# One searched order for all five engines, zero matmuls at the start, and half copies by DMA, in a chunk-selecting attention with a gated MLP

## The chip, the core and the metric

The kernel runs on one core of one Trainium2 chip. A core has a matrix engine (TensorE, PE in the profile; its weight loads are PEld), a vector engine (VectorE, DVE), a scalar engine (ScalarE, ACT), GpSimd (POOL) and SyncE (SP), which here only issues DMA transfers. The engines run side by side, each through its own queue in order, and wait for each other on semaphores. On-chip memory is SBUF; TensorE writes its results to PSUM, which has eight banks. The metric is the device time of the whole program in microseconds.

## The reference, cut to what matters

The input is q, k and v of shape (4, 8, 768, 64): batch, heads, tokens, head dimension. Attention looks at six of the 24 chunks of 32 keys, chosen for each query by an upper bound of its scores in the chunk.

```python
k_min, k_max = chunk minima and maxima of k            # 24 chunks of 32 keys
ub = sum(maximum(q * k_min, q * k_max), axis=-1)       # (B, H, S, 24)
ub = where(causal, ub, -1e9)
top_chunks = argsort(ub)[..., -6:]
scores = q @ k.T / 8
scores = where(selected chunk and causal, scores, -1e9)
attn = softmax(scores)
x = attn @ v                                           # heads side by side: (4, 768, 512)

h = maximum(x @ w_in, 0)                               # (4, 768, 1024)
u, v = h[..., :512], h[..., 512:]
v_n = (v - mean(v)) / sqrt(var(v) + 1e-6)
v_s = w_spatial @ v_n + b_spatial                      # over the tokens
out = (u * v_s) @ w_out                                # (4, 768, 512), float32
```

## The kernel before

The kernel works on 16 pairs of heads, four pairs to a batch. A pair goes through preparation (transposes, bounds, selection), scores, exp, values and normalisation. When the four pairs of a batch are done, its MLP is mixed with the attention of the batches that follow.

The selection is folded into the scores matmul. The operand of a head, `kh`, has the transposed k in 64 partitions and in the other 64 the constant `expand`, which is -30000 where a chunk's row meets that chunk's keys. The other operand, `a`, has q and, for each chunk, a one where the chunk was not selected. So both heads of a pair come from one 128-partition transpose and are then split in halves.

```python
def k_transpose(self):                      # six 128x128 transposes into a PSUM bank
    ...
def k_max(self):                            # DVE, from PSUM; k_min likewise, negated
    nc.vector.tensor_reduce(self.kmm[:, 0, :], self.kT..., axis=AX.X, op=Alu.max)

def k_bounds(self):                         # two copies of 64 partitions
    for hi, (d0, d1) in enumerate(HALF):
        copy = nc.gpsimd.tensor_copy if 2 <= self.i < 4 else nc.scalar.copy
        s0, s1 = HALF[1 - hi]
        copy(self.km[d0:d1, :, hi], self.kmm[s0:s1])

def k_operand(self, hi):                    # half of kT, PSUM -> kh, once for each head
    d0, d1 = HALF[1 - hi]
    copy = nc.scalar.copy if self.i < 1 else nc.vector.tensor_copy
    copy(self.kh[hi][d0:d1], self.kT[d0:d1])

def bounds(self):
    mm(ub[:, 0:(NQT - 1) * W], lhsT=sub_chunk, rhs=later, start=True, stop=False)   # 240 columns
    for qi in range(1, NQT):
        for m in range(2):
            mm(ub[:, (qi - 1) * W:qi * W], lhsT=self.rq[:, m, ...], rhs=self.km[:, m]..., ...)

# then: ten MAX8 on DVE, select() (DVE, is_lt against the sixth), transposes of q with the selection
# into PSUM, and a_copy() by ACT or DVE; from pair 8 on one DMA transpose does both

def scores(self, hi, g):                    # 12 groups a pair, three PSUM banks
    for si, (t, q0, n, col) in enumerate(TILES[g]):
        mm(sc[:, col:col + n], lhsT=self.kh[hi][:, t * P:(t + 1) * P], rhs=self.a[...], ...)
    nc.scalar.activation(out=self.e[hi][...], in_=sc[:, 0:width], func=Act.Exp, scale=scale)
```

Loads of q, k, v and the weights are issued by GpSimd and convert float32 to float16. The k and q buffers and the v buffers are rings of three. `kh` is a ring of four.

```python
for hi, (d0, d1) in enumerate(HALF):        # init_kh: the constant half, on ACT
    nc.scalar.copy(kh_ring[i][hi][d0:d1, :], expand)
```

The order comes from a table of "beats": each step is put at a beat, and the steps are issued beat by beat. Only for the first beats is the order of TensorE's queue kept as written; everywhere else a scheduler may move instructions.

```python
at(t0 - 22, p.k_max)
at(t0 - 21, p.q_transpose)
at(t0 - 20, p.k_min)
... (cut)
with tc.manual_schedule(engines={mybir.EngineType.PE}):
    for beat in sorted(b for b in beats if b < 6):
        ...
for beat in sorted(beats):
    ...
```

Of the kernel before, what the change touches and what calls it, by code (L numbers as in the profile page):

```python
# [16 lines left out]
P = 128  # L17
CHUNK = 32
# [28 lines left out]

@with_exitstack
def kernel(
# [12 lines left out]
    B, H, S, D = q.shape  # L62
# [4 lines left out]
    NQT = S // P  # L67
    NDO = DM // P
    KO = DH // P
    HP = H // 2  # L70
    NPAIR = B * HP
    CPT = P // CHUNK
    scale = 1.0 / math.sqrt(D)
    mm = nc.tensor.matmul

# [4 lines left out]
    ps_sc = ctx.enter_context(tc.psum_pool(name="ps_sc", bufs=3))  # L80
    ps_tr = ctx.enter_context(tc.psum_pool(name="ps_tr", bufs=1))
    ps_acc = ctx.enter_context(tc.psum_pool(name="ps_acc", bufs=1))
    ps_ml = ctx.enter_context(tc.psum_pool(name="ps_ml", bufs=3))

    def ml_tile():
        return ps_ml.tile([P, 512], F32, tag="mlp", name="mlp")
# [3 lines left out]

    BEATS = 12
    beats = defaultdict(list)

    def at(beat, fn, *args):
        beats[beat].append((fn, args))

    HALF = ((0, D), (D, 2 * D))


    NB = 4
    v_ring = [ring.tile([P, 4, NQT, D + 2], F16, name=f"vt{i}") for i in range(3)]
    qs_ring = [ring.tile([P, 2, NQT, 4, D], F16, name=f"qs{i}") for i in range(3)]
    km_ring = [ring.tile([P, 2, 2, NCH], F16, name=f"km{i}") for i in range(2)]
    kh_ring = [[ring.tile([P, S], F16, name=f"kh{i}_{hi}") for hi in range(2)] for i in range(NB)]
    identity = cp.tile([P, P], F16)
    tri = cp.tile([P, P], F16)
    sub_chunk = cp.tile([P, P], F16)
    later = cp.tile([P, (NQT - 1) * 2 * NCH], F16)  # L110
    expand = cp.tile([D, S], F16)
    eps_t = cp.tile([P, 1], F32)

    def init_identity():
        nc.vector.memset(identity, 0.0)
        nc.gpsimd.affine_select(out=identity, in_=identity, compare_op=Alu.not_equal, fill=1.0,
                                base=0, channel_multiplier=1, pattern=[[-1, P]])

    def init_ring(i):

        nc.vector.memset(qs_ring[i][:, :, :, 0:4:3, :], 0.0)

    def init_small():
        nc.vector.memset(km_ring[0], 0.0)
        nc.vector.memset(km_ring[1], 0.0)
        nc.vector.memset(eps_t, 1e-6)
        for t in v_ring:
            nc.vector.memset(t[:, :, :, D:D + 2], 1.0)

    def init_expand():  # L130

        nc.vector.tensor_scalar(expand.rearrange("d (c s) -> d c s", s=CHUNK),
                                in0=identity[0:D, 0:NCH].unsqueeze(2).to_broadcast([D, NCH, CHUNK]),
                                scalar1=NEG, scalar2=None, op0=Alu.mult)
        nc.vector.tensor_copy(sub_chunk.rearrange("d (c s) -> d c s", s=CHUNK),
                              identity[:, 0:CPT].unsqueeze(2).to_broadcast([P, CPT, CHUNK]))

    def init_masks():

        nc.gpsimd.memset(later, 0.0)  # L140
        lv = later.rearrange("p (t h c) -> p t h c", h=2, c=NCH)
        nc.gpsimd.affine_select(out=lv, in_=lv, compare_op=Alu.is_ge, fill=NEG, base=CPT,
                                channel_multiplier=1, pattern=[[CPT, NQT - 1], [0, 2], [-1, NCH]])
# [4 lines left out]
    def init_kh(i):  # L148
        for hi, (d0, d1) in enumerate(HALF):
            nc.scalar.copy(kh_ring[i][hi][d0:d1, :], expand)  # L150


    W = 2 * NCH
    xT = {}
    tiles = {}

    class Pair:
        def __init__(self, i):
            self.i = i
            self.b, self.hp = divmod(i, HP)  # L160
            self.heads = [4 * (self.hp // 2) + self.hp % 2 + 2 * hi for hi in range(2)]
            self.qs = qs_ring[i // 2 % 3][:, i % 2]
            self.kh, self.km = kh_ring[i % NB], km_ring[i % 2]
            self.e = {}

        def k_transpose(self):
            if self.i < 16:
                self.kT = kT = ps_ml.tile([P, S], F16, tag="mlp", name="kTp")
                for t in range(NQT):
                    nc.tensor.transpose(kT[:, t * P:(t + 1) * P], self.k[:, t], identity)  # L170
            else:
                self.kT = sb.tile([P, S], F16, tag="kT", name="kT", bufs=3)
                nc.sync.dma_start_transpose(out=self.kT.rearrange("d (t s) -> d t s", s=P),
                                            in_=self.k.rearrange("p t h d -> p (t h d)"))

        def k_max(self):
            self.kmm = sb.tile([P, 2, NCH], F16, tag="kmm", name="kmm")
            nc.vector.tensor_reduce(self.kmm[:, 0, :], self.kT.rearrange("d (c ch) -> d c ch", ch=CHUNK),  # L178
                                    axis=AX.X, op=Alu.max)

        def k_min(self):
            nc.vector.tensor_reduce(self.kmm[:, 1, :], self.kT.rearrange("d (c ch) -> d c ch", ch=CHUNK),  # L182
                                    axis=AX.X, op=Alu.min, negate=True)

        def k_bounds(self):
            for hi, (d0, d1) in enumerate(HALF):
                copy = nc.gpsimd.tensor_copy if 2 <= self.i < 4 else nc.scalar.copy
                s0, s1 = HALF[1 - hi]
                copy(self.km[d0:d1, :, hi], self.kmm[s0:s1])

        def k_operand(self, hi):
            d0, d1 = HALF[1 - hi]
            copy = nc.scalar.copy if self.i < 1 else nc.vector.tensor_copy
            copy(self.kh[hi][d0:d1], self.kT[d0:d1])  # L194

        def trans_tile(self):

            if self.b == 0:
                return ps_ml.tile([P, S], F16, tag="mlp", name="trm")
            return ps_tr.tile([P, S], F16, tag="tr", name="tr")  # L200

        def q_transpose(self):
            self.tr = self.trans_tile()
            for t in range(1, NQT):
                nc.tensor.transpose(self.tr[:, t * P:(t + 1) * P], self.qs[:, t, 1:3, :], identity)  # L205

        def q_parts(self, m):
            if m == 0:
                self.rq = sb.tile([P, 2, S], F16, tag="rq", name="rq")
                nc.vector.tensor_scalar(self.rq[:, 0, P:S], in0=self.tr[:, P:S], scalar1=0.0, scalar2=None, op0=Alu.max)  # L210
            elif self.i < 1:
                nc.scalar.activation(self.rq[:, 1, P:S], self.tr[:, P:S], func=Act.Relu, scale=-1.0)
# [4 lines left out]
        def bounds(self):  # L217
            ub = self.ub = ps_tr.tile([P, 512], F32, tag="tr", name="ub")
            mm(ub[:, 0:(NQT - 1) * W], lhsT=sub_chunk, rhs=later, start=True, stop=False)
            for qi in range(1, NQT):  # L220
                for m in range(2):
                    mm(ub[:, (qi - 1) * W:qi * W], lhsT=self.rq[:, m, qi * P:(qi + 1) * P],  # L222
                       rhs=self.km[:, m].rearrange("p h c -> p (h c)"), start=False, stop=(m == 1 and qi == NQT - 1))

        def top(self, step):
            ub = self.ub
            if step == 0:
                self.max8 = sb.tile([P, NQT - 1, 2, 8], F32, tag="max8", name="max8")
            for qi in (1, 2, 3) if step == 0 else (4, 5):
                for hi in range(2):  # L230
                    c0 = (qi - 1) * W + hi * NCH
                    nc.vector.max(self.max8[:, qi - 1, hi, :], ub[:, c0:c0 + CPT * (qi + 1)])  # L232

        def select(self):
            flat = self.qs[:, 1:NQT]
            sel = bass.AP(flat.tensor, flat.offset, [list(flat.ap[0]), [4 * D, NQT - 1], [3 * D, 2], [1, NCH]])
            nc.vector.tensor_tensor(sel, in0=self.ub[:, 0:(NQT - 1) * W].rearrange("p (t h c) -> p t h c", h=2, c=NCH),
                                    in1=self.max8[:, :, :, TOPK - 1:TOPK].to_broadcast([P, NQT - 1, 2, NCH]),
                                    op=Alu.is_lt)

        def a_transpose(self, hi):
            if hi == 0:
                self.a = sb.tile([P, NQT, 2, P], F16, tag="a", name="a")
            if self.i >= 8:
                if hi == 0:
                    nc.sync.dma_start_transpose(out=self.a.rearrange("d t h s -> d (t h) s"),
                                                in_=self.qs.rearrange("p t c d -> p (t c d)"))
                return
            self.tr = self.trans_tile()
            for t in range(NQT):  # L250
                nc.tensor.transpose(self.tr[:, t * P:(t + 1) * P], self.qs[:, t, 2 * hi:2 * hi + 2, :], identity)  # L251

        def a_copy(self, hi):
            if self.i >= 8:
                return
            copy = nc.vector.tensor_copy if self.i < 2 and hi == 0 else nc.scalar.copy
            copy(self.a[:, :, hi, :], self.tr.rearrange("d (t s) -> d t s", s=P))  # L257


        def scores(self, hi, g):  # L260
            if g == 0:
                self.e[hi] = sb.tile([P, EW], F16, tag="e", name="e", bufs=3)
            self.sc = sc = ps_sc.tile([P, 512], F32, tag="sc", name="sc")
# [6 lines left out]
            width = sum(n for (_, _, n, _) in TILES[g])  # L270
            nc.scalar.activation(out=self.e[hi][:, g * 512:g * 512 + width], in_=sc[:, 0:width], func=Act.Exp, scale=scale)  # L271

        def triangle(self, hi):
            if self.b == 0:
                return
# [5 lines left out]


        def values(self, hi, blocks, first=False, last=False):
            if first:
                av = ps_acc.tile([P, 512], F32, tag="acc", name="acc")
                self.av = av[:, 0:NQT * (D + 1)].rearrange("p (t c) -> p t c", c=D + 1)
            for n, (t, qi) in enumerate(blocks):
                c = block_column(t, qi)
                mm(self.av[:, qi, :], lhsT=self.e[hi][:, c:c + P], rhs=self.v[hi][:, t, 0:D + 1],  # L289
                   start=first and n == 0, stop=last and n == len(blocks) - 1)  # L290

        def normalise(self, hi):
            if hi == 0:
# [301 lines left out]
```

The softmax here doesn't subtract the row's maximum and nothing guards it: scores larger than these inputs give would overflow.

## Time and profile before

| | |
|---|---|
| time, median of 3 | 208.82 us (208.65 to 209.14) |
| span of the profiled execution | 206.9 us |
| chain of waits, by engine | PE 69%, ACT 17%, DVE 8%, issue 2%, DMA 2% |
| software DMA queue (GpSimd's loads) | 76,544 packets, 12.20 MB |
| hardware DMA queue (SyncE's transfers) | 37,856 packets, 14.75 MB |
| exp, 192 instructions on ACT | 96.9 us busy |
| longest waits in sum | POOL on ACT's exp 66.3 us, ACT's output copy on PE 19.1 us, ACT's exp on PE's scores 13.4 us |

How to read the page: the first part gives each engine's busy time. The second cuts the span into 40 slices, about 5.2 us each here; a digit is the busy share in tenths. A group line gives source line, engine, operation, output and inputs, shapes and count, then busy time and the mean of one, then idle time ahead of the group and what ended it. Matmuls are pipelined: a 512-column matmul shows 379 ns, while the next one starts well before its end. So a mean is no pitch, and the pitch has to be taken from runs of matmuls. Idle time of GpSimd costs nothing here by itself, since it is ahead of its work.

### The profile page before, as it was taken

The page shows a single profiled execution, that of the slowest core. Times are in us where ns is not written, and L with a number is a line of the kernel's source. Part 1 is how long each engine was busy: PE and PEld are TensorE (multiplying, and loading weights), DVE is VectorE, ACT ScalarE, POOL GpSimd, SP SyncE. Part 2 cuts the span into 40 slices and gives each one's busy share as a digit, 9 for nine tenths or more (in the row PEclk, how much of TensorE's full clock was granted, in tenths as well). Part 3 has the DMA queues.
Part 4 walks back from the last instruction along what each step waited for, and adds up shares of the span by engine and source line. Part 5 has one row for each costly group of instructions (what it writes and reads, how often), then busy time and mean ns, then how long its engine had stood idle before and what let it go on. Part 6 is the DMA issues. An engine that isn't in the chain of part 4 may idle for free.

```text
span 206.9 us, 5068 instructions
## 1 busy us (share of the span) xinstructions
PE 187.8 (91%) x1922; PEld 115.1 (56%) x1922; DVE 154.5 (75%) x454; ACT 158.1 (76%) x326; POOL 80.5 (39%) x100
## 2 busy tenths in 40 slices
PE   0368999898899999999999999999999999999992
PEld 0266776775666665656655656565555454444440
DVE  6467979989799989899797999887647456365520
ACT  4797989899998889785989996669999830666042
POOL 7997659596992463236114111111111110000000
PEclk9999999999999999999999999999999999999999
DMA  5999999999999999979998926648782124540356
GB/s 38 92 118 154 140 178 158 173 177 167 177 162 162 97 119 128 135 130 147 149 278 153 180 62 57 127 88 158 181 166 65 38 29 92 187 152 3 72 128 256
DMA packets 114424, 27.27 MB, mean 132 GB/s; under 512 B 109536, under 2 KB 110816, under 8 KB 114400
## 3 DMA queue, kind: packets, MB, share of 16 engines
q0 software_dynamic: 76544, 12.20, 89.8%
q1 hardware_dynamic: 37856, 14.75, 36.4%
q8 instruction: 15, 0.25, 0.5%
q14 instruction: 9, 0.07, 0.1%
HBM read 24.38 MB, written 6.29 MB: 148 GB/s over the span
## 4 chain that ended last, share of the span: by engine, by line
PE 69%; ACT 17%; DVE 8%; issue 2%; DMA 2%; POOL 0%; DVEq 0%; ACTq 0%; POOLq 0%
PE mlp L388 40%; PE sc L266 12%; ACT e L271 10%; PE acc L289 7%; PE kTp L170 2%; ACT a L257 2%; DVE kmm L178 2%; PE ub L222 2%; DMA k<-in_k_dram 2%; PE trm L251 2%; ACT vraw L398 1%; PE tr L205 1%; DVE vn L412 1%; DVE kmm L182 1%; ACT u L420 1%
## 5 line engine op out<-in xcount | busy, mean ns | idle before, releaser
L271 ACT ACTIVATE e<-sc 128x512 f16<-128x512 f32 x192 | 96.9, 553 | 14.8 <-PE sc L266 13.4
L266 PE MATMUL sc<-a,kh 128*128 128x512 f16 (+3 forms) x256 | 65.5, 308 | 2.1 <-ACT e L271 1.5
L388 PE MATMUL mlp<-w_in_sb,xT 128*128 128x512 f16 x192 | 53.0, 379 | 0.1
L278 POOL TENSOR_SCALAR_AFFINE_SELECT e<-e 128x768 f16<-128x768 f16 x24 | 20.9, 869 | 66.3 <-ACT e L271 66.3
L289 PEld LDWEIGHTS <-e 128*128 128x128 f16 x672 | 31.4, 97 | 17.0 <-DVE x L297 3.8
L388 PE MATMUL mlp<-vn,wsT 128*128 128x512 f16 x144 | 37.3, 379 | 0.0
L289 PE MATMUL acc<-vt,e 128*128 128x65 f16 x672 | 35.3, 193 | 0.7 <-DVE x L297 0.4
L266 PEld LDWEIGHTS <-kh 128*128 128x128 f16 x256 | 22.7, 98 | 13.3 <-issue 0.8
L437 ACT COPY o<-mlp 128x512 f32<-128x512 f32 x24 | 14.1, 586 | 19.5 <-PE mlp L388 19.1
L400 DVE BATCH_NORM_STATS2 stats<-vraw 128x6 f32<-128x512 f32 x24 | 16.6, 693 | 12.9 <-ACT vraw L398 12.5
L388 PE MATMUL mlp<-w_out_sb,gT 128*128 128x512 f16 x96 | 25.1, 379 | 0.0
L388 PEld LDWEIGHTS <-xT 128*128 128x128 f16 x192 | 17.2, 97 | 12.6 <-issue 0.4
L427 DVE SCALAR_TENSOR_TENSOR g<-mlp,b_col,u 128x512 f16<-128x512 f32 x24 | 17.9, 748 | 7.3 <-PE mlp L388 6.2
L232 DVE MAX8 max<-ub 128x8 f32<-128x8 f32 (+4 forms) x160 | 15.6, 165 | 5.1 <-PE ub L222 4.9
L388 PEld LDWEIGHTS <-wsT 128*128 128x128 f16 x144 | 12.9, 98 | 10.4
L178 DVE TENSOR_REDUCE kmm<-kTp 128x24 f16<-128x768 f16 x16 | 15.2, 948 | 3.7 <-PE kTp L170 2.7
L297 DVE TENSOR_TENSOR x<-acc,rec 128x384 f16<-128x384 f32 x32 | 17.6, 551 | 0.4
L336 POOL DMA_DIRECT2D qs<-in_q_dram x14 | 14.6, 1049 | 5.9 <-PE sc L266 5.9
L194 DVE COPY kh<-kTp 64x768 f16<-64x768 f16 x30 | 16.5, 549 | 0.5
L398 ACT ACTIVATE vraw<-mlp 128x512 f32<-128x512 f32 x24 | 14.4, 601 | 3.0 <-PE mlp L388 3.0
L420 ACT ACTIVATE u<-mlp 128x512 f16<-128x512 f32 x24 | 14.3, 598 | 1.7 <-PE mlp L388 1.5
L327 POOL DMA_DIRECT2D k<-in_k_dram x14 | 14.4, 1045 | 2.5 <-PE kTp L170 1.8
(67 smaller groups left out, 230.2 us busy)
## 6 DMA issues: line engine op xcount, KB each, us to landing
out_dram<-o SPq DMA_DIRECT2D x24, 256.0 KB, 2.3
vt<-in_v_dram POOLq DMA_DIRECT2D x8, 384.0 KB, 8.8
k<-in_k_dram POOLq DMA_DIRECT2D x14, 192.0 KB, 8.1
qs<-in_q_dram POOLq DMA_DIRECT2D x14, 192.0 KB, 7.5
ws_raw<-in_moe_w_spatial_dram POOLq DMA_DIRECT2D x6, 192.0 KB, 6.9
w_in_sb<-in_moe_w_in_dram POOLq DMA_DIRECT2D x8, 128.0 KB, 6.9
w_out_sb<-in_moe_w_out_dram POOLq DMA_DIRECT2D x4, 128.0 KB, 7.9
k<-in_k_dram POOLq DMA_DIRECT2D x4, 96.0 KB, 3.4
```

The source lines that it names most:

```text
L178: nc.vector.tensor_reduce(self.kmm[:, 0, :], self.kT.rearrange("d (c ch) -> d c ch", ch=CHUNK), axis=AX.X, op=Alu.max)
L194: copy(self.kh[hi][d0:d1], self.kT[d0:d1])
L266: mm(sc[:, col:col + n], lhsT=self.kh[hi][:, t * P:(t + 1) * P], rhs=self.a[:, q0 // P:(q0 + n) // P, hi, :], start=True, stop=not diag)
L271: nc.scalar.activation(out=self.e[hi][:, g * 512:g * 512 + width], in_=sc[:, 0:width], func=Act.Exp, scale=scale)
L278: nc.gpsimd.affine_select(out=blk, in_=blk, compare_op=Alu.is_ge, fill=0.0, base=0, channel_multiplier=-1, pattern=[[0, NQT], [1, P]])
L289: mm(self.av[:, qi, :], lhsT=self.e[hi][:, c:c + P], rhs=self.v[hi][:, t, 0:D + 1], start=first and n == 0, stop=last and n == len(blocks) ...
L297: nc.vector.tensor_tensor(self.x16[:, :, hi, :], in0=self.av[:, :, 0:D], in1=rec.to_broadcast([P, NQT, D]), op=Alu.mult)
L388: mm(st[group][:, 0:cols], lhsT=lhsT, rhs=rhs, start=(j == 0), stop=(j == n - 1))
L398: nc.scalar.activation(st["vraw"][:, ti, :], h, func=Act.Relu)
L400: nc.vector.bn_stats(stats, st["vraw"][:, ti, :])
L420: nc.scalar.activation(st["u"][:, ti, :], h, func=Act.Relu)
L427: nc.vector.scalar_tensor_tensor(g, in0=vs, scalar=b_col[:, ti:ti + 1], in1=st["u"][:, ti, :], op0=Alu.add, op1=Alu.mult)
```

## The change

The new kernel keeps the mathematics and changes who does what and when.

- **One order for every engine.** The beats are gone. Every step has a name, and one list (`ORDER`, 1,437 names) gives the sequence; the scheduler is switched off for all engines, so every queue is fixed. The list was found by a local search in a replay model of the engines, whose source is kept in the file. The model's numbers also choose the engine of some copies (`flip`).
- **Zero matmuls.** 50 matmuls of a zero tile (`dm0` to `dm49`) stand in TensorE's queue among the first steps, 21 of them ahead of the first transpose of k. Their result is not read. They are meant to bring TensorE to its full clock before data come.
- **k is copied once** (pairs 2 to 15): one 128x768 copy out of PSUM, by DVE or ACT, frees the bank; two DMA copies issued by SyncE put its halves into `kh`.
- **Bounds** go into `km` with one DVE multiply against a mask of the own head, in place of two half copies by ACT.
- **The late mask** of the bounds covers only each query tile's own chunks: 40 columns, not 240.
- **The first pairs**: k of pairs 0 and 1 and q of pair 0 are transposed twice, into two banks, so that two engines can read them at the same time; pair 0's selection and its transposes are split in parts.
- **Rings** of k, q and v have four places.

```diff
+PLAN = {'late': 40, 'mlp_first': 8, 'qbuf': 4, 'kbuf': 4, 'vbuf': 4, 'kcp': 2, 'dum': 50, 'warm0': 6.6,
+        'flip': ['ac10', 'ac31', 'ac50', 'ac51', 'kc10', 'kc11', 'kc15', 'kc4', 'kc5', 'kc8', 'kc9',
+                 'oc05', 'oc11', 'oc12', 'oc14', 'oc15', 'oc22']}
+ORDER = """
+id0 small id1 ring2 lk000 ring0 lk010 expand lq000 dz ring3 kh30 dm14 dm46 dm36 dm18 lq010 dm28 ring1 dm11 dm33 dm34
+kh00 dm4 dm6 dm35 lk001 dm13 dm15 dm9 dm42 kh10 dm12 dm24 dm0 dm7 lk011 dm26 dm2 kT0 kh21 lq011 dm45 dm23 dm21 dm1
... (cut: 1,437 names in all)
+"""
-    later = cp.tile([P, (NQT - 1) * 2 * NCH], F16)
+    later = cp.tile([P, (NQT - 1) * 2 * CPT], F16)
+    act("dz")(lambda: nc.vector.memset(idle_op, 0.0))
... (cut)
+        def k_transpose_again(self):
+            self.kTb = ps_acc.tile([P, S], F16, tag="acc", name="kTb")
+            for t in range(NQT):
+                nc.tensor.transpose(self.kTb[:, t * P:(t + 1) * P], tiles["k", self.g][:, self.i % 2][:, t], identity)
+        def k_copy(self, engine):
+            kT = sb.tile([P, S], F16, tag="kT", name="kT", bufs=3)
+            copier(engine)(kT, self.kT)
+            self.kTp, self.kT = self.kT, kT
         def k_bounds(self):
-            for hi, (d0, d1) in enumerate(HALF):
-                copy = nc.gpsimd.tensor_copy if 2 <= self.i < 4 else nc.scalar.copy
-                s0, s1 = HALF[1 - hi]
-                copy(self.km[d0:d1, :, hi], self.kmm[s0:s1])
+            nc.vector.tensor_tensor(self.km, in0=self.kmm.unsqueeze(2).to_broadcast(shape),
+                                    in1=own_head.unsqueeze(1).unsqueeze(3).to_broadcast(shape), op=Alu.mult)
-        def k_operand(self, hi):
-            d0, d1 = HALF[1 - hi]
-            copy = nc.scalar.copy if self.i < 1 else nc.vector.tensor_copy
-            copy(self.kh[hi][d0:d1], self.kT[d0:d1])
+        def k_operand(self, engine, hi):
+            (d0, d1), (s0, s1) = HALF[hi if self.packed else 1 - hi], HALF[hi]
+            dst, src = self.kh[hi][d0:d1], getattr(self, "kTb", self.kT)[s0:s1]
+            if engine == "SP":
+                nc.sync.dma_start(out=dst, in_=src)
+            else:
+                copier(engine)(dst, src)
... (cut)
+    for n in range(prm["dum"]):
+        @act(f"dm{n}")
+        def warm(n=n):
+            if "warm" not in tiles:
+                tiles["warm"] = ps_sc.tile([P, 512], F32, tag="sc", name="warm")
+            mm(tiles["warm"][:, 0:P], lhsT=idle_op, rhs=idle_op, start=True, stop=True)
... (cut)
-    with tc.manual_schedule(engines={mybir.EngineType.PE}):
-        for beat in sorted(b for b in beats if b < 6):
-            for fn, args in beats.pop(beat):
-                fn(*args)
-    for beat in sorted(beats):
-        for fn, args in beats[beat]:
-            fn(*args)
+    with tc.manual_schedule():
+        for name in ORDER.split():
+            acts[name]()
```

Names in the order: `lk`, `lq`, `lv` loads; `kT`, `qT` transposes; `kmax`, `kmin` reductions; `kc` the one k copy; `kop` a half of `kh`; `ub` the bounds matmuls; `top`, `sel` maxima and selection; `sc`, `ex`, `av` scores, exp and values, with pair, head and part; `v`, `u`, `s`, `o` the matmul groups of the MLP.

## The prediction

> **What bounds the kernel now.** I read the busy totals first, then the slices, then a table of stages, then the timeline where the stages meet. From the page:
>
> ```profile
> PE 187.8 (91%) x1922; PEld 115.1 (56%) x1922; DVE 154.5 (75%) x454; ACT 158.1 (76%) x326; POOL 80.5 (39%) x100
> ...
> PE   0368999898899999999999999999999999999992
> ...
> DVE  6467979989799989899797999887647456365520
> ACT  4797989899998889785989996669999830666042
> ...
> DMA  5999999999999999979998926648782124540356
> ```
>
> TensorE (PE) is full from slice 16 on. Before that VectorE (DVE), ScalarE (ACT) and the DMA engines all stand at 8 to 9. So there are two regimes, and I cut the span where they meet. I chose the cuts from the timeline: first matmul 5.75, first exp 15.29, first matmul of the MLP 55.09. Columns of the stage table: stretch, its length, busy time (and count) of PE, weight loads, DVE, ACT, POOL, then clock, DMA share, GB/s.
>
> ```profile
> 0.00:5.70 5.70, 0.00 (x0) 0.00 (x0) 3.34 (x12) 2.81 (x3) 4.51 (x10) 1.00 0.66 42
> 5.70:15.30 9.60, 5.27 (x46) 4.14 (x47) 5.54 (x17) 8.35 (x14) 9.60 (x14) 1.00 1.64 105
> 15.30:55.40 40.10, 35.92 (x523) 26.83 (x521) 35.04 (x114) 36.16 (x79) 30.70 (x40) 1.00 2.25 165
> 55.40:80.00 24.60, 23.98 (x292) 15.98 (x291) 23.32 (x78) 21.98 (x47) 15.32 (x17) 1.00 2.04 136
> 80.00:202.60 122.60, 122.22 (x1066) 68.16 (x1065) 87.27 (x237) 88.04 (x187) 20.38 (x22) 1.00 0.82 123
> ```
>
> Busy PE is not peak PE, since matmuls overlap. So I count the streaming work. The chain of waits gives the pitch:
>
> ```profile
> 171.50 31.53 PE mlp L388 x146
> ```
>
> 31.53/146 = 0.216 us for 512 columns; six 128-column transposes in 0.34 us give 0.056; 21 value matmuls in 0.65 give 0.030. From 55.1 on the groups of instructions count 432 MLP matmuls (93.2), scores 64x512, 22x384, 44x256, 44x128 (24.7), 483 value matmuls (14.4), 159 transposes (8.9) and the bounds (about 3.8): **144.9 us** of work in 151.8 us. The rest, 6.9, is 4.1 of tail (last matmul 202.8, then copy and store) and only about 2.8 of gaps. After the first MLP matmul there is nearly nothing to win. Whatever the change gains has to come from moving that matmul forward from 55.1.
>
> Why is it at 55.1? The head:
>
> ```profile
> 5.75 0.80 PE L170 MATMUL kTp<-identity,k 128*128 128x128 f16 x6 [5.75 <-DMA k<-in_k_dram]
> ...
> 14.35 0.63 PE L266 MATMUL sc<-a,kh 128*128 128x512 f16 x1
> ...
> 15.29 0.60 ACT L271 ACTIVATE e<-sc 128x512 f16<-128x512 f32 x1
> ```
>
> Six transposes take 0.80 (0.51 for six at 54.5) and a 512-column matmul 0.63 (0.38 later), so TensorE runs at half clock until about 16.5, although the page's clock row reads 9 throughout. Then come 40 us with ACT 36.2 busy and DVE 35.0: 90% and 87%. Neither is full, but each waits for the other in turn, and loads back up beside them (issued at 16 to 20, two k loads took 10.0 us to land against 3.2 for the first).
>
> **What the Trainium skill says.** (1) "TensorE: Matmul & The Clock Gate", Part 1: the array starts at half clock and is released after about 4 us of sustained activity, in a free-running window of about 3.4 us; an idle window throttles it again. The trace agrees: slow at 14.35, fast at 17.9, after PE became dense at 12.6. (2) The same page, "Back-to-back issue gap": N/2.4 + 2.5 ns, 215.8 for 512; the trace has 216. (3) "PSUM — Partial Sum Buffer", Terms: two engines may not touch one bank at once, reads included. The trace has ACT's first kh copy waiting until 8.50 for DVE's second reduction of the same bank; this is why the change transposes the first k and q twice. (4) "DMA: Bandwidth & Descriptors", "Issuing engines are not separate DMA queues": SyncE's copies share the 16 engines with GpSimd's loads. No copy of this kind is in this trace; the xT transposes from SyncE take 2.7 to 8.8 us to land, so the claim is plausible here.
>
> **The change, part by part.**
>
> *k copied once, halves by SyncE (pairs 2 to 15).* The present cost:
>
> ```profile
> L194 DVE COPY kh<-kTp 64x768 f16<-64x768 f16 x30 | 16.5, 549 | 0.5
> ...
> L189 ACT COPY km<-kmm 64x48 f16<-64x48 f16 x28 | 6.4, 229 | 0.6
> ```
>
> A pair has two half copies on DVE (pitch about 0.47) and two bound copies on ACT. After: one 128x768 copy of 0.52, on DVE for seven pairs and on ACT (0.7) for seven, and one small DVE multiply (about 0.2) for the bounds. DVE: 28 x 0.47 = 13.2 out, 7 x 0.52 + 16 x 0.2 = 6.8 in. ACT: 6.4 out, 7 x 0.7 = 4.9 in. 28 DMAs of 96 KB (2.75 MB on top of 27.27) come in; PE work is unchanged.
>
> *Late mask.* `later` shrinks from 240 columns to 40: 16 x (0.103 - 0.028) = 1.2 us of PE, of which 0.75 after the first MLP matmul.
>
> *Doubled transposes, split select, 50 zero matmuls (head only).* 17 extra transposes, 0.95 us, in idle PE time. The zeros need a memset that stands behind two ring fills and `expand` on DVE, about 4.0; 21 of them stand ahead of k's transpose: 21 x 0.107 = 2.25 at half clock, so to 6.3. On GpSimd the identity (0.32) now goes ahead of the k loads, so k lands at about 6.05 instead of 5.75. k's transpose starts near 6.35, still slow; warm by about 8. Then DVE does both reductions (to about 8.95), q's positive part (9.1 to 9.5), the bounds, and also pair 1's two reductions (to 11.8) ahead of pair 0's maxima. The bounds matmul waits for `later`, now after ten loads on GpSimd: 1.65 + 8 x 0.88 + 2 x 1.05 = 10.8, plus 0.5. Maxima 11.95 to 13.05, select, the first a-copies 14.4 to 15.15, first score 15.2, **first exp near 15.5**. So the head gains nothing at its end (15.29 before), but pair 1 is ready by about 18 where its select ended at 21.3.
>
> *Order and balance of all engines.* Between the first exp and the first MLP matmul I count the new order by the rows' pitches. ACT: 60 exps of pairs 0 to 4 at 5.3 us a pair (10 x 0.495 + 2 x 0.17) = 26.5, half a microsecond of pair 5, six a-copies x 0.69 = 4.1, two k copies 1.4: **32.5** against 36.2 now. DVE: 12 reductions x 0.88, 10 q parts x 0.40, five pairs of maxima and selects 6.4, three a-copies 1.3, four k copies 2.1, eight normalisations 4.6, three x copies 1.4, bounds 1.0: **31.4** against 35.0. Both lose about 3.6 us in the same place. Taken pair by pair, with whichever engine has more in each, it is 33.6 us; I do not expect that from real queues. At 93% of 32.5 the stretch is 34.9, so the first MLP matmul comes at 15.5 + 34.9 = **50.4** in place of 55.1.
>
> *After it.* Work 144.9 - 0.75, tail 4.1, gaps 2.8 in the present order. The new order was searched for in a model and leaves every queue fixed, with little slack; I put 3.0 to 3.5. Sum: 50.4 + 144.1 + 4.1 + 3.2 = 201.8 in the profile; the time is 1.9 above the span before (208.8 against 206.9), so 203.7. The fixed order may also close gaps that I left in the 93%; I take **203.2**.
>
> **Rivals.**
> (a) *DMA becomes the bound.* The order brings weights and k, q, v much earlier. Up to the last w_in load ahead of the first MLP matmul GpSimd has issued about 6.2 MB, with about 1 MB of SyncE copies beside it. At the 165 GB/s of the third row, with 0.75 MB landed by 10 us: (7.2 - 0.75)/0.165 = 39 us, so 49 us. That is level with the compute estimate. v for pair 0 is now issued behind all of k and q of pair 2 and would land at 19.5 to 20.5, when its first value matmuls are due. For: the DMA row at 9. Against: GpSimd is busy in most of that stretch, so part of the 165 is issue. Cost 2 to 4 us, about 205.5.
> (b) *Fixed queues stall in the steady part.* Each SyncE copy sits in one queue with transposes of about 1.2 to 1.9 us; gT transposes took 5.1 us at 70 to 100 us against 2.5 later. A late one stops PE, which never leaves its order. For: stage four has DVE at 95%. Against: from 80 us DVE and ACT are at about 71%. Cost 2 to 6 us, 205 to 208.5.
> (c) *The plan comes true*: 33.6 us per pair sum and gaps under 1.5 us. Time 199.5 to 200.5.
> (d) *The zeros delay k.* At most 0.3 to 0.6 us, inside the range.
>
> **Range and chances.** Head and order are near 203; (a) and (b) pull up, (c) down by 3. I give 199.6 to 207.0. Two per cent is 4.2 us, 204.6. I put 0.66 below, 0.28 within 2% (mostly (a) or a mild (b)), 0.06 slower by over 2%, for which fixed queues would have to cost over 9 us.
>
> **What would show it.** Right: first exp at 15 to 16, first MLP matmul at 49 to 52, ACT and DVE above 92% in between, PE busy 99% after 80 us, scores of 0.38 from the first one on. DVE's total falls to about 147 and ACT's to about 150. Wrong: a wait of PE or ACT on the DMA of v, q or kh at the head of the waits (rival a), PE idle over 4 us between 55 and 200 (rival b), or cold matmuls after 15 us because the zeros leave an idle window.

## The result and the profile after

The changed kernel takes **211.23 us** (median of 4 runs, 209.77 to 212.23) against 208.75 for the kernel before: a ratio of 1.0112, 95% interval 1.0069 to 1.0156. It is slower by about one per cent; the prediction was 203.2 with a range up to 207.0. The profiled execution has a span of 208.1 us. All ratios here leave out executions more than 1.5% above the fastest of the same kernel, so a ratio can differ from that of two medians.

From the page of the changed kernel, first the busy totals, then the slices of 5.2 us:

```profile
PE 188.9 (91%) x1989; PEld 118.8 (57%) x1989; DVE 151.6 (73%) x463; ACT 149.2 (72%) x297; POOL 79.8 (38%) x96
...
PE   1977999879999999996979999999999999999992
...
DVE  7598999668889997899676978794574747265520
ACT  5698899839799967775777896668789930566032
...
PEclk9999999969999999999999999999999999999999
DMA  6999999999999998999898999787484016435257
```

ACT has lost 8.9 us of work and DVE 2.9, and the kernel got no faster: the engines do less and stand still more. Slices 7 and 8 (36 to 47 us) have DVE at 6, ACT once at 3, and the clock row drops to 6. The DMA row is at 8 to 9 for longer than before. TensorE has a second dent in slices 18 to 20 (94 to 109 us), where it was full before.

The table of stages, cut at the first exp and at 54.88, where the chain of waits enters the MLP (stretch, length, busy time and count of PE, weight loads, DVE, ACT, POOL, then clock, DMA, GB/s):

```profile
15.54:54.88 39.34, 34.06 (x517) 26.75 (x516) 33.38 (x116) 33.42 (x68) 25.22 (x31) 0.96 2.30 166
54.88:204.00 149.12, 144.95 (x1353) 83.19 (x1350) 106.44 (x303) 103.90 (x214) 40.33 (x44) 1.00 1.12 141
```

The first exp comes at 15.54. The timeline has the first MLP matmul at 54.72, only 0.4 us before the 55.09 of the kernel before. ACT is busy for 33.4 of 39.3 us, 85%, where it had 90% with more to do.

What TensorE waits for, in sum (engine, line, releaser: us in total, times, longest), from the list of waits:

```profile
PE warm L857 <- DVE idle_op L553: 4.2, 1, 4.2
PE sc L794 <- DMA kh<-kT: 4.0, 3, 2.1
PE sc L794 <- DMA a<-qs: 2.0, 1, 2.0
```

The first line is the start and costs nothing by itself. The other two are new: six microseconds in four stops. The largest stop in the chain of waits (start us, us, what):

```profile
35.75 7.33 DMA kh<-kT
...
43.13 0.39 PE sc L794
...
44.65 0.43 PE sc L794
45.08 0.11 PE sc L797
...
46.82 1.09 ACT e L803 x2
```

A half copy of pair 3 (`kop31`) is issued at 35.75 and lands 7.33 us later. TensorE started its last matmul before it at 40.81 and stands for 2.1 us. The lead of the copy was short for a second reason: the list has `kop31` behind `kop51` and `kop50` in SyncE's queue, and these wait for pair 5's k, which ScalarE copies from 33.68 on, while pair 3's own k was copied at 25.11. After the stop a 512-column scores matmul holds TensorE for 0.43 us, twice the 0.216 of full clock: the trace's clock records show half clock from 43.47 to 46.88, 3.41 us. The list of DMA issues (KB each, median us to landing) has the copy beside the loads:

```profile
k<-in_k_dram POOLq DMA_DIRECT2D x14, 192.0 KB, 8.0
qs<-in_q_dram POOLq DMA_DIRECT2D x14, 192.0 KB, 7.6
kh<-kT SPq DMA_DIRECT2D x28, 96.0 KB, 6.0
```

Two later stops, again from the chain of waits:

```profile
90.58 8.13 DMA a<-qs
...
107.02 2.02 DMA kh<-kT
```

The first is the transpose of pair 9's selection, which SyncE issues; TensorE stands from 96.9 to 98.8 for it. The second has another nature. In the list, `kop131` (a half of pair 13) stands ahead of `sc914`, the last scores group of pair 9 on that head, and both pairs share one slot of the `kh` ring. So the copy waits until the group before it is done (107.02), and `sc914` waits for the copy and reads pair 13's keys. That one group of 192 is thus computed with other keys than in the kernel before, so here the change does not keep the mathematics. The copy takes 2.0 us of the chain, and TensorE stands still for 1.5 of them.

### The profile page after: what moved, and what is told of

It is laid out like the page before. It is cut to its first block, busy times and chain, and to the rows that moved or that the text cites. A ratio compares the mean times of both kernels' runs of the same rounds, so it can differ in the third digit from the quotient of the medians.

```text
span 208.1 us, 5191 instructions
## 1 busy us (share of the span) xinstructions
PE 188.9 (91%) x1989; PEld 118.8 (57%) x1989; DVE 151.6 (73%) x463; ACT 149.2 (72%) x297; POOL 79.8 (38%) x96
## 4 chain that ended last, share of the span: by engine, by line
PE 64%; DMA 17%; POOL 8%; ACT 7%; issue 1%; SPq 1%; DVE 0%; ACTq 0%
PE mlp L914 40%; PE sc L794 12%; DMA kh<-kT 8%; PE acc L820 7%; DMA qs<-in_q_dram 4%; DMA a<-qs 4%; ACT e L803 4%; POOL k L573 2%; POOL qs L588 2%; POOL qs L579 1%; POOL k L588 1%; SPq L699 1%; PE ub L726 1%; ACT a L784 1%; PE trq L706 1%
## 5 line engine op out<-in xcount | busy, mean ns | idle before, releaser
L803 ACT ACTIVATE e<-sc 128x512 f16<-128x512 f32 (+1 forms) x192 | 93.9, 559 | 23.2 <-PE sc L794 19.3
L794 PE MATMUL sc<-a,kh 128*128 128x512 f16 (+3 forms) x256 | 63.1, 309 | 6.4 <-DMA kh<-kT 4.0
L914 PE MATMUL mlp<-w_in_sb,xT 128*128 128x512 f16 x192 | 51.2, 379 | 0.0
L809 POOL TENSOR_SCALAR_AFFINE_SELECT e<-e 128x768 f16<-128x768 f16 x24 | 21.4, 892 | 75.5 <-ACT e L803 55.5
L820 PE MATMUL acc<-vt,e 128*128 128x65 f16 x672 | 36.2, 194 | 0.8 <-DMA vt<-in_v_dram 0.8
L670 DVE TENSOR_REDUCE kmm<-kTp 128x24 f16<-128x768 f16 x32 | 29.7, 949 | 2.7 <-PE kTp L649 2.2
L914 PE MATMUL mlp<-w_out_sb,gT 128*128 128x512 f16 x96 | 26.1, 379 | 0.0
L936 DVE BATCH_NORM_STATS2 stats<-vraw 128x6 f32<-128x512 f32 x24 | 16.1, 681 | 9.1 <-ACT vraw L931 9.0
L968 ACT COPY o<-mlp 128x512 f32<-128x512 f32 x18 | 10.4, 589 | 12.8 <-PE mlp L914 12.1
L951 DVE TENSOR_SCALAR vn<-vraw,mv,rstd 128x512 f16<-128x512 f32 x24 | 13.2, 594 | 2.2 <-ACT rstd L978 2.2
```

The costliest lines, as they stand in the source:

```text
L670: nc.vector.tensor_reduce(self.kmm[:, m, :], src.rearrange("d (c ch) -> d c ch", ch=CHUNK), axis=AX.X, op=op, negate=(m == 1))
L809: nc.gpsimd.affine_select(out=blk, in_=blk, compare_op=Alu.is_ge, fill=0.0, base=0, channel_multiplier=-1, pattern=[[0, NQT], [1, P]])
L820: mm(self.av[hi][:, qi, :], lhsT=self.e[hi][:, c:c + P], rhs=self.v[hi][:, t, 0:D + 1], start=first and n == 0, stop=last and n == len(blo ...
L914: mm(st[kind, ti], lhsT=lhsT, rhs=rhs, start=(j == 0), stop=(j == n - 1))
L936: nc.vector.bn_stats(st["stats", ti], st["vraw"][:, ti, :])
```

## The experiments

Two theories. **L, latency:** the list was searched with transfers of 2 to 4 us; on the chip they take 6 to 8 us, TensorE's queue is in order, so it stops. **R, rest of the work:** ScalarE and VectorE limit the stretch to 55 us, and the stops are only where that shows. Beside them: the zeros (Z) and the fixed queues as such (F).

### VectorE makes the half copies

```diff
+    engine.update({n: "DVE" for n in engine if n.startswith("kop") and engine[n] == "SP"})
```

> The changed kernel with one thing undone: the 28 half copies into kh are made by VectorE from the SBUF copy of k (64x768, one estimated 0.3 us each, so about 8.4 us more on VectorE) instead of by SyncE as DMA. Names and order stay. Theory L (late halves: SyncE's copies share the DMA engines with the loads, take 6 us and more instead of about 2, and the searched order places them just in time, so TensorE stops): the waits on kh by DMA are gone, no pause of 2.3 us at 41 us and so no stretch at half clock after it, first MLP matmul near 51 in place of 54.9, time 204.5 to 206.5. Rival F (the fixed order loses time at every deviation, loads and VectorE above all, and the copies are only where it shows): other waits take their place, VectorE's extra work is felt, time 209 to 212.

Measured: 210.30 us (208.93 to 211.83), ratio 1.0078 (1.0059 to 1.0096). The stop at 41 us and the half clock after it are gone, but 28 copies of 0.355 us put 9.9 us more on VectorE. Table of stages:

```profile
25.00:40.00 15.00, 12.62 (x209) 10.20 (x206) 14.86 (x51) 13.12 (x27) 10.86 (x14) 1.00 2.34 157
```

VectorE is busy 14.86 of 15 us. One limit was exchanged for another (first MLP matmul 54.1). The time is in the range of F and not in that of L, but VectorE has new work, so the run does not separate the theories.

### SyncE's half copies as early as the data allow

Same list, but each `kop` name stands right behind the copy of k that it reads or the last reader of its slot, whichever comes later.

> The changed kernel with SyncE's half copies kept, but each put as early as it may go: right after the copy of k, or after the last scores that read the ring place. In the changed kernel the copy for pair 3's second head stands behind two copies of pair 5, so it is issued at 35.7 though its k was there ten microseconds before. Theory L: a latency of 6 to 7 us does no harm when the copy is issued early; pauses at 41 and at 72 go, half clock too; time 205.5 to 208. If the copies themselves (2.75 MB more on busy DMA engines) slow the loads, it stays near 210. Rival F: 209 to 211.

Measured: a median of 211.91 us over 20 runs, from 207.04 to 214.91; the ratio, 0.9991 (0.9966 to 1.0015), rests on five of them. So neither a gain nor a loss is shown, and the median misses L's range. In the profiled run the copy of pair 3 is issued at 26.1 in place of 35.75, the stop at 41 us and its half clock are gone though the copies land no sooner (7.3 us in the median from 25 to 45 us), and the first MLP matmul comes at 52.7. Pair 9's transpose now takes longest (chain of waits):

```profile
90.33 8.90 DMA a<-qs
99.37 0.59 PE sc L794
```

TensorE stands 3.7 us before 99.37, and the clock records show half clock for 6.8 us from 98.25 on (0.59 for the scores after it in this line). Where the copy is early the stop vanishes, as L says; the loss moves to the next late transfer.

### Without the zero matmuls

```diff
-dz ... dm14 dm46 dm36 ...        (51 names taken out of the list)
```

> The changed kernel without the 50 zero matmuls and their memset. They brought the full clock at 9.3 us instead of about 16.6. Without them k's transpose starts about 0.3 us earlier (6.05 instead of 6.38), but the work up to about 15 us runs at half clock: six transposes 0.85 in place of 0.50, the bounds 0.54 in place of 0.40. I expect the first exp at 16 to 16.5 instead of 15.54 and a time 0 to 1 us longer, 210.5 to 212.5. If the first exp hangs on VectorE alone, no difference.

Measured: 210.14 us (208.48 to 211.56), ratio 1.0065 (1.0039 to 1.0091). Full clock comes at 15.4 us rather than 9.3 and the first exp at 16.3 instead of 15.5, as expected, yet the end is no later: the time lies just below the expected 210.5 to 212.5. In this change the zeros buy nothing that the time shows.

### Zeros inside the stop

```diff
+            if (self.i, hi, g) == (3, 1, 0):
+                for _ in range(40):
+                    mm(sc[:, 0:P], lhsT=idle_op, rhs=idle_op, start=True, stop=True)
```

> The changed kernel with 40 zero matmuls of 128 columns (2.2 us at full clock) put in front of the first scores of pair 3's second head, the place where TensorE stands still from 40.8 to 43.1. They write the bank that these scores then overwrite, so nothing else moves. Rival C (the half clock after that pause, 43.5 to 46.9, costs time): the clock stays full, the time falls by 1 to 2 us to about 209.5 and its scatter gets smaller. If ScalarE and VectorE set the pace in that stretch, the clock costs nothing: within 0.4 us of the changed kernel.

Measured: 212.22 us (210.45 to 213.07), ratio 1.0147 (1.0095 to 1.0200), so neither expectation came true. The 40 zeros fill 2.23 us from 41.06 on and the half clock at 43 is gone. But pair 9's transpose then takes 10.2 us, TensorE stops 3.4 us at 95.7, and half clock follows there (100.5 to 103.9). Taking the first half clock away brought no gain; what a half clock costs by itself is not shown, since the later stop is longer in this run.

### One half copy behind its slot's last reader

```diff
-sc915 av901 sc913 ex911 av902 kop131 o04.0 va11 x8 sc914 ex915
+sc915 av901 sc913 ex911 av902 o04.0 va11 x8 sc914 kop131 ex915
```

> One name of the order is moved: the copy kop131 (pair 13's second half into the kh slot that pair 9 still uses) stands behind sc914 in place of ahead of it. In the changed kernel the queue of TensorE stops from 107.02 to 109.08 us there: the last scores group of pair 9 waits for a copy that could not be issued before 107.02. Theory L (the order leaves too little time between issue and need): the 2.0 us are on the chain, and the time falls by 1.5 to 2.0 us, to 209.2 to 209.7. Rival R (VectorE and ScalarE are the limit all over, TensorE's pauses are only where they show): the stop moves to a later place and the time stays at 210.7 to 211.7.

Measured: 211.21 us (210.39 to 212.79), ratio 1.0123 (1.0076 to 1.0171), in the range of R. The stop at 107 is gone, but in the profiled run the two stops ahead of it, which the edit doesn't touch, are longer than in the changed kernel: 2.6 us at 41 and 3.6 at 97, against 2.1 and 2.0.

```profile
91.47 9.21 DMA a<-qs
```

The 2.0 us did not show in the time. The two profiles differ by 0.5 us in the one stop and by 1.6 in the other, which the edit doesn't explain; the run doesn't say where the 2.0 us went.

### The half copies left out

```diff
             if engine == "SP":
-                nc.sync.dma_start(out=dst, in_=src)
+                if self.i < 4:
+                    nc.sync.dma_start(out=dst, in_=src)
```

The scores of pairs 4 to 15 use the k halves of pairs 0 to 3, and 24 copies of 96 KB are not made.

> SyncE's half copies of pairs 4 to 15 are left out (24 DMAs; kh keeps the halves of pairs 0 to 3, so the scores of the later pairs use those keys); all else as in the changed kernel. Theory L: the stops on kh go (2.3 us at 41, 0.6 at 72, 2.0 at 107) and the half clock from 43.5 to 46.9 with them (some 1.7 us of work lost), the one on the transposes of pair 9 at 97 stays or shortens. First MLP matmul at 51 to 52.5, time 204 to 206.5. Rival R: first MLP matmul still after 54, with ScalarE or VectorE busy over 93% from 30 to 50 us, time 208.5 to 210.5.

Measured: **203.61 us** (203.48 to 204.91), ratio 0.9764 (0.9730 to 0.9798). The first MLP matmul (form, count, duration, first and last start):

```profile
L915 PE MATMUL mlp<-w_in_sb,xT x12: 378/379/379, 50.8 to 54.6; 128*128 128x512 f16 x12
```

It comes at 50.8, where the profiles with SyncE's copies at their places in the list have it at 52.6 to 55.1, and no half clock is left between the start and the tail. The stretch from near the first exp to there:

```profile
15.50:50.50 35.00, 32.53 (x514) 25.49 (x513) 32.99 (x119) 33.11 (x68) 24.34 (x31) 1.00 2.34 166
```

ScalarE is busy for 33.1 of 35.0 us, 95%. This decides between L and R: with the work of ScalarE, VectorE and TensorE unchanged, the copies cost 211.23 - 203.61 = 7.6 us, the half clock after their stop and the stop on `kop131` included. The time is a little better than L had it. It also speaks against F, since every queue is fixed here too.

### The weight loads left out

```diff
-        nc.gpsimd.dma_start(out=w_in_sb[...], in_=moe_w_in[...])
+        nc.gpsimd.memset(w_in_sb[...], 0.01)          # likewise w_spatial, w_out
```

> The 18 loads of w_in, w_spatial and w_out are left out (GpSimd writes constants into the tiles instead, so the MLP multiplies constants); loads of q, k, v and all transfers of SyncE stay. Theory C (the half copies take 7 us because they share the DMA engines with the loads): the median landing of kh copies between 25 and 45 us falls from 7 to under 4.5 us, the stop at 41 shrinks by over 1 us, and the first MLP matmul comes at 52 to 53.5; time 207.5 to 209.5. Rival Q (the copies are slow by themselves or by standing behind each other in SyncE's own queue): landing stays at 6 to 8 us and the time at 210.5 to 212.

Measured: 210.43 us (208.16 to 212.62), ratio 1.0055 (1.0034 to 1.0075). Landing of the half copies issued from 25 to 45 us, from the answer on tile kh:

```profile
DMA to landing us min/median/max: 5.8/7.6/8.2
```

7.6 us, no better than with the weights (7.3), so the expectation of C failed here, and the stop at 41 us grew to 3.3. But the test was weak: GpSimd issued the q, k and v loads sooner in their place, and the DMA engines still moved 145 GB/s in this window against 171. So the next run takes nearly all loads away.

### Nearly all loads left out

Only the loads of pairs 0 and 1 and the bias stay; q, k, v of the other pairs and the weights are constants that GpSimd writes. Everything that SyncE transfers stays.

> All of GpSimd's loads are left out except those of pairs 0 and 1 and the small bias; GpSimd writes constants into the tiles at the same places in its queue, so all later scores and the MLP work on constants. The order and every transfer of SyncE stay. With the weights alone left out, the loads of q, k and v moved forward and filled the gap, so that run told nothing on the stop at 41 us. Theory C (the 6 to 8 us of a half copy are the loads' packets ahead of it on the shared DMA engines): kh copies land in 2 to 3 us everywhere, the stops at 41, 97 and 107 us shrink to under 0.7 us each, there is no half clock after 17 us, and the span is 196 to 201 us. Rival Q (the copies are slow in themselves, or by SyncE's own queue): they land in 6 to 8 us still and the span stays at 206 to 210.

Measured: **201.87 us** (2 runs, 201.81 and 201.94), ratio 0.9649 (0.9603 to 0.9695). The stage from 25 to 45 us, of the changed kernel and then of this one, each with the landing of the half copies issued in it:

```profile
25.00:45.00 20.00, 16.48 (x264) 13.15 (x261) 16.29 (x56) 16.62 (x34) 11.63 (x16) 0.96 2.30 171
```

```profile
DMA to landing us min/median/max: 6.0/7.3/8.4
```

```profile
25.00:45.00 20.00, 19.01 (x305) 15.19 (x304) 19.49 (x71) 19.61 (x40) 11.70 (x15) 1.00 0.15 37
```

```profile
DMA to landing us min/median/max: 2.0/2.2/2.5
```

The same seven copies take 2.2 us at 37 GB/s and 7.3 at 171. VectorE and ScalarE then are busy 97% and 98% of the time, and the first MLP matmul starts at 49.2. The copy is not slow in itself, nor is SyncE's queue: the loads beside it are what makes it late. C's ranges hold, but for the stop on `kop131`, which is still there, 1.5 us, since that is a matter of the list.

### A new search with the measured landing times

Only the list differs. In the replay model each transfer gets the extra time seen on the chip, and the local search runs again from the old list, with `kop131` behind its slot's last reader.

> Only the list ORDER differs from the changed kernel: a new local search in the same replay model, with the same engines, instructions and zeros, but with the landing times measured on the chip: kh copies 4.2 us more than the model had up to 100 us, 2.0 more up to 125, 0.5 after; other SyncE transfers 3 us more up to 115 and 1 after; loads 5 us more from 16 to 48 and 2 more up to 110. With these numbers the model puts the searched order of the changed kernel at a span of 209.4 to 210.3 (without them 196.9), near the chip's 208.1 to 211, and the new list at 198.8, or 202 to 203 with the times disturbed at random. Theory L (the order was searched against transfers that are too short; the mechanism of the change is sound): time 201 to 206, first MLP matmul at 50 to 52.5. Rival M (the model misses other things as well, and any order searched in it disappoints): 208 to 212.

Measured: 211.60 us in the median of four runs, one of 205.73 and three of 210.76 to 212.58. The expectation of L is missed by the median. The profile, of the 205.73 run, has no stop on `kh` and starts the MLP at 51.3. Its clock row shows a new loss:

```profile
PEclk9958999999999999999999999999999999999997
```

Half clock in slices 2 and 3, 10 to 20 us: the search had put 41 of the 50 zeros ahead of k's transpose, where the changed kernel has 21, so that fewer were left for the waits that follow. The model has no clock that falls again. But this run, with its half clock, was the fastest of the four; what held the other three up is not shown, as there is no profile of them.

> As the run before it in this set, searched in the same way, but with the 50 zero matmuls left out of the list (its own search, so its order differs too). The model's span is 198.8. Theory L: 201 to 206.5. If the zeros help once the stops are gone, it is 0.5 to 1.5 us slower than the list with zeros; if they do nothing, within 0.7 us of it.

Measured, the same search without zeros: **207.30 us** (205.90 to 210.15), ratio 0.9886 (0.9836 to 0.9936) from three of the four runs; the first MLP matmul at 52.2 and no wait on `kh` in the list of waits. It is outside the expected 201 to 206.5 but in the median faster than both kernels. Its order differs too, so the zeros' share in the difference of the two lists isn't separated.

### Only TensorE's order fixed

```diff
-    with tc.manual_schedule():
+    with tc.manual_schedule(engines={mybir.EngineType.PE}):
```

> The changed kernel with the scheduler on again for every engine but TensorE: the order of TensorE stays to the instruction, those of VectorE, ScalarE, GpSimd and SyncE are the scheduler's. Rival F (it is the fixed queues as such that lose time, because a blocked instruction blocks all behind it on its engine): 205 to 209. Theory L (TensorE's own order with its too short lead is what stops): the stops at 41 and 97 stay where the transfers are issued no earlier, 209.5 to 214.

Measured: 229.28 us (227.92 to 230.29), ratio 1.0937 (1.0885 to 1.0990), worse than either theory had it. The list of waits of TensorE:

```profile
PE acc L820 <- POOL e L809: 10.0, 2, 5.0
PE sc L794 <- DMA kh<-kT: 4.3, 1, 4.3
PE kTp L649 <- DMA k<-in_k_dram: 3.9, 2, 3.1
```

So freeing the other queues under TensorE's list is no help: the scheduler's orders serve that list worse. Together with the two fixed lists that took 203.6 and 201.9 us once the copies or the loads were gone, this leaves little of F.

### A second search

The latencies of the run without zeros, over the model's own: kh copies 5.0 us up to 100 and 3.0 up to 125, the other SyncE transfers 1.5 to 3.5, loads 6 and then 3; scored as the mean of three drawings.

> A second search from the list without zeros, now with the landing times seen in that run: kh copies 5.0 us over the model's figure up to 100 us and 3.0 up to 125, the a and xT transposes 3.5 up to 125, gT 1.5 up to 115, loads 6 from 16 to 48 us and 3 up to 112, and scored as the mean of three drawings of these delays. The model gives a span of 198.0, and 201 to 203 with the delays drawn at random. Theory L: the waits of TensorE on transfers after 55 us fall below 1.5 us in sum, first MLP matmul at 51 to 52.5, time 204 to 207, below the 207.3 of the first search without zeros and below the kernel before. Rival M (the model misses other costs, so that a better list in it is none on the chip): 207 to 210.

Measured: **206.34 us** (204.38 to 207.81), ratio 0.9855 (0.9819 to 0.9891), in the expected range. All six runs are below the lowest of the kernel before (208.33). One transfer still comes late in the profiled run (chain of waits):

```profile
93.17 11.44 DMA a<-qs
```

So the waits after 55 us were not below 1.5 us as expected: this one stops TensorE for 3.1. The three runs of a mean clock of 0.995 and above took 204.4 to 205.6, the three below 0.99 took 207.1 to 207.8.

## Why the prediction was wrong

| step | predicted | measured |
|---|---|---|
| first matmul of the zeros; of k | 4.0; 6.35 us | 4.17; 6.38 |
| full clock | about 8 | 9.3 |
| first exp | 15.5 | 15.54 |
| ACT's work up to the first MLP matmul | 32.5 | 33.4 |
| DVE's work up to there | 31.4 | 33.4 |
| **its share, 93%; first MLP matmul** | **50.4** | **85%; 54.72** |
| work after it | 144.1 | 143.4 |
| **gaps after it** | **3.2** | **5.9** |
| tail | 4.1 | 4.1 |
| span | 201.8 | 208.1 |

(The gaps are start distances beyond columns/2.4 + 2.5 ns, at least 28 ns, between the first MLP matmul and the last matmul; the work is the rest of those 149.3 us. Counted in the same way, the kernel before has 3.5 us of gaps, and the one without the half copies 3.7.)

- **Failed: "At 93% of 32.5 the stretch is 34.9, so the first MLP matmul comes at 15.5 + 34.9 = 50.4."** The reduction of work was real, but utilisation fell to 85%. The missing term stands one part earlier, in "28 DMAs of 96 KB (2.75 MB on top of 27.27) come in": they were entered as bytes, with no time from issue to need. They take 7.3 us where the loads run. Without them ScalarE's share is 95%, the first MLP matmul comes at 50.8 and the time is 203.6; without the loads it comes at 49.2. So the estimate of the compute was nearly right (0.9 us short for ACT, 2.0 for DVE), and of the missing 4.3 us, 3.9 went with the late copies and the half clock behind them.
- **Failed: gaps "I put 3.0 to 3.5".** They were 5.9: 2.1 us for pair 9's transpose, 1.6 for `kop131` and 1.3 between 70 and 80 us, 0.6 of it for a late `kh` copy.
- **Rival (b), "fixed queues stall", was the right one and got too little.** Its evidence lay in the profile before: transfers of SyncE took 2.7 to 8.8 us to land. The prediction quoted that range and then charged the copies nothing. It also looked for the stall in the steady part; the larger one came before it. Rival (a) named the DMA as a bound by bytes, 49 us; the loss came not from bytes, but from how long a small copy waits among them: from 25 to 45 us the kernel before moves the same 171 GB/s as the changed one, without a stop.
- **Half right: DVE's total "about 147".** It is 151.6. The plan's `flip` list gives VectorE six output copies of 0.69 us, 4.1 us, that the sum left out; they lie after 117 us, off the path. ACT's 149.2 met "about 150".
- **Right:** the head's end, the late mask, the tail, "the head gains nothing at its end", and scores of 0.38 from the first one on. Full clock came 1.3 us later than written, the first exp on time nonetheless. **"The zeros delay k" by at most 0.6:** the time says no more than that they don't help.
- The prediction named "a wait of PE on the DMA of v, q or kh at the head of the waits" as the sign that it was wrong. That line is there, for kh.

What stays open: how far the spread of the runs (209.8 to 212.2 here, 207.0 to 214.9 with early half copies, 208.3 to 209.6 in 47 runs of the kernel before) is the landing times and how far the clock that falls after a stop. And no run took pair 9's transpose away by itself.

## What to carry to other kernels

A copy handed from a compute engine to a DMA queue isn't free because the queue is idle: enter its time from issue to landing as it is while the loads run, and ask whether the in-order reader can wait so long. A list searched in a model is only as good as its longest-latency numbers: here the same model with measured landing times, and without the zeros, turned +1.1% into -1.5% (by the medians of all runs, +1.2% into -1.1%). When a reduction of work leaves the time unchanged, leave out the suspect with everything else in place; one such run showed what five smaller edits had not.

## What was unexpected in the hardware

- **A small copy waits behind big loads.** 96 KB from SBUF to SBUF: 2.2 us at 37 GB/s, 7.3 at 171 GB/s. The Trainium skill, "DMA: Bandwidth & Descriptors", section "Anatomy of one DMA — SWDGE (gpsimd) path", fits 2.0 us plus bytes over 436 GB/s for a transfer issued by GpSimd, by which 98,304 bytes would be 2.2 us, an estimate. The copies from SyncE without the loads agree with it (2.2); beside them the measurement decides, at more than three times that.
- **A stop of 2.1 us was enough for half clock, and a stop of 3.3 us was not.** The skill's page "TensorE: Matmul & The Clock Gate", Part 1, has the array fall back after an idle window of about 3.4 us. The length of the slow stretch agrees, 3.41 us; the stop was shorter than such a window. Within each trace here the clock changes only at moments a whole number of 3.41 us steps apart (in the changed kernel at 9.34, 43.47 and 46.88, ten steps and one), so one can look at how busy TensorE was in each step. First the changed kernel, with the stops at 41 and 97 us, then the run without the weight loads, with its stop of 3.3 us at 40.6 (columns as in the tables of stages):

```profile
40.06:43.47 3.41, 1.31 (x26) 1.02 (x24) 1.68 (x4) 1.68 (x3) 1.63 (x3) 1.00 2.83 144
43.47:46.88 3.41, 3.41 (x38) 2.56 (x36) 2.16 (x14) 1.95 (x5) 2.05 (x2) 0.50 3.11 159
94.67:98.08 3.41, 2.21 (x27) 1.25 (x25) 3.13 (x18) 2.33 (x5) 0.76 (x1) 1.00 2.57 149
```

```profile
38.74:42.16 3.42, 1.85 (x31) 1.57 (x29) 1.28 (x3) 2.51 (x5) 3.42 (x5) 1.00 2.35 152
42.16:45.57 3.41, 1.67 (x32) 1.30 (x33) 1.95 (x9) 1.03 (x3) 0.55 (x1) 1.00 3.21 135
45.57:48.98 3.41, 3.21 (x49) 2.45 (x48) 3.38 (x14) 3.38 (x7) 0.00 (x0) 1.00 1.09 92
```

The step with the stop of 2.1 us had TensorE busy for 38%, and half clock followed. The stop at 97 left 65%. The stop of 3.3 us fell across two steps of 54% and 49%, and none followed. So in these traces the place of a stop counted beside its length, with a limit near half. It is no sharp rule: in the first new search a step of 52% was followed by half clock.
- **Copies of k:** 128x768 out of PSUM took 0.55 us on VectorE and 0.83 on ScalarE; 64x768 within SBUF 0.355 on VectorE, against 0.549 out of PSUM in the kernel before.
